# Second expert layer: where expert 1's rows are transposed, and how far the row buffers of the later experts may run ahead

## The chip, the core and the metric

The kernel runs on one core of a Trainium2 chip. The metric is the device time of one execution in microseconds, median of the runs shown. Engines: TensorE (PE), VectorE (DVE), ScalarE (ACT), GpSimd (POOL), SyncE (SP). SP computes nothing here: it issues most of the DMAs, in program order.

## What is computed

The reference is an attention (4 batches, 8 heads, 576 positions, head size 64, with a local window in four heads and a dilated one in the other four), then a first expert layer (8 experts, one expert per token, tokens with a negative skip score are left out), then a second one in which each of the 2304 tokens goes to two of eight experts. The change lies in the second layer:

```python
top2 = np.argpartition(-noisy_logits, 2, axis=1)[:, :2]
...
for e in range(E):                      # E = 8
    for k in range(2):
        mask = top2[:, k] == e
        h = np.maximum(x[mask] @ w1[e], 0.0)          # x: 512 wide, w1[e]: 512 x 1024
        out[mask] += top2_w[mask, k, None] * (h @ w2[e])   # w2[e]: 1024 x 512
```

## The kernel before

**Tiling.** Each expert of the second layer gets 608 slots for its rows, as five tiles: four of 128 rows and one of 96 (`rows2`). fp32 products are made of three passes with operands split into a high and a low part (`mm3`, lines 437 to 441; the split is `split`, lines 431 to 434: ACT writes the high part, DVE or POOL subtracts). For an expert `e` TensorE first makes the hidden values (`hidden2`, line 1437): eight blocks `f`, each in two column ranges `g` (256 and 352 rows), and after each of them ACT and then DVE write the high and low hidden values (lines 1445 and 1446, tiles `hh2`, `hl2`). Then it makes the output of the five row tiles (`product2`, line 1449): 24 matmuls of 512 columns each in one of two `pt` banks, which ACT empties into `y2` (two buffers, line 1460), from where POOL issues a scattered add into the output (line 1216). Expert 0 makes the columns `g` = 1 of its hidden values after the products of its first two row tiles, and expert 7 takes the halves in the other order.

**Rows of an expert.** A tile's rows are gathered by an indirect DMA of POOL (`fetch`, line 1257) into one of four `xg2` buffers. Matmuls need them transposed.
- Expert 0: four TensorE transpositions per tile into a `tp` bank, then a split (`turn`, line 1289).
- Experts 1 to 7: `put` (line 1266) writes the gathered tile to a DRAM tile `xq`, `spread` (line 1273) reads it back with four DMAs of SP into an `xs2` buffer (three of them), 32 partitions each, and `turn_v` (line 1293) transposes blocks of 32 x 32 on DVE into the one `xt2` buffer; the split of that tile follows with the next call. The weights' rows are read in another order for these experts (line 706, `p k` in place of `k p`) so that the permuted rows fit.

**What sets the order.** `P.step` (line 485) cuts the weights into parts between the matmuls; three raw buffers `wraw` are loaded ahead by SP. While expert `e` is worked on, `ready` (line 1505) calls `put`, `fetch` and `spread` for tiles 0 to 2 of expert `e + 1` during its hidden values, and `next_rows` (line 1553) calls `turn_v` and `spread` for the rest during its products, at `f` = 1 and 5. TensorE's order is as written. The order of all other engines is made by a scheduler that takes whatever its model has ready; every engine then works through its own list in order, and an instruction that waits holds up what stands behind it. The `xq` tiles are made anew for each expert, so a `put` waits for no earlier `spread`.

Of the kernel before, what the change touches and what calls it, by code (L numbers as in the profile page):

```python
# [8 lines left out]
F32 = mybir.dt.float32  # L9
# [3 lines left out]
ALU = mybir.AluOpType  # L13
AF = mybir.ActivationFunctionType
# [416 lines left out]
def split(nc, hi, lo, src, eng=None):  # L431

    nc.scalar.activation(hi, src, AF.Copy)  # L433
    (eng or nc.vector).tensor_tensor(out=lo, in0=src, in1=hi.bitcast(F32), op=ALU.subtract)  # L434


def mm3(nc, out, a, b, start, stop):

    nc.tensor.matmul(out, lhsT=a[0], rhs=b[0], start=start, stop=False)  # L439
    nc.tensor.matmul(out, lhsT=a[0], rhs=b[1], start=False, stop=False)  # L440
    nc.tensor.matmul(out, lhsT=a[1], rhs=b[0], start=False, stop=stop)  # L441
# [71 lines left out]
def piece(w1, w2, e, i, dims="o (k p) f -> p (o k) f"):  # L513

    if i < 2:
        src = w1[e:e + 1] if isinstance(e, int) else w1[bass.ds(e, 1)]
        return src.rearrange(dims, p=128)[:, :, 512 * i:512 * i + 512]
    src = w2[e:e + 1] if isinstance(e, int) else w2[bass.ds(e, 1)]
    return src.rearrange("o (f p) d -> p (o f) d", p=128)[:, 4 * (i - 2):4 * (i - 2) + 4, :]
# [3 lines left out]
def tile_attention_moe_moe(ctx, tc, q, k, v, w_skip, w_gate, w1, w2, v_gate, v_noise, noise, u1, u2, out):  # L523
    nc = tc.nc
    B, H, S, D = q.shape
    N, DM = B * S, H * D
    E, F = w_gate.shape[1], w1.shape[2]
# [16 lines left out]
    NS, NA, CAP = 5, 2, 608  # L544
    rows2 = [min(128, CAP - 128 * i) for i in range(NS)]
# [7 lines left out]
    def bank(tag):  # L553
        return ps_pool.tile([128, 512], F32, name=tag, tag=tag, bufs=nbufs[tag])

    cp = ctx.enter_context(tc.tile_pool(name="const", bufs=1))
    dr = ctx.enter_context(tc.tile_pool(name="dr", bufs=1, space=DRAM))
# [141 lines left out]
    every2 = [2, 2, 8, 2, 2, 4, 2, 1]  # L699
    P = Pieces(tc, raw_p)  # L700
    for kk, src in order:
        P.plan(kk, src, every1.get(kk[1]))
    for e in range(E):
        for i in range(4):

            P.plan((2, e, i), lambda e=e, i=i: piece(u1, u2, e, i, f"o ({'p k' if e else 'k p'}) f -> p (o k) f"), every2[e])

    def busy(n):

# [5 lines left out]
    def gather(xg, idx, n):  # L715
        gather.last = nc.gpsimd.indirect_dma_start(out=xg, out_offset=None, in_=xs[:n, :],  # L716
                                                   in_offset=bass.IndirectOffsetOnAxis(ap=idx, axis=0))
        return xg

    def transposed(xg, hi, lo, n=128):  # L720
        ps = bank("tp")
        for c in range(KC):
            nc.tensor.transpose(ps[:, 128 * c:128 * c + n], xg[:n, 128 * c:128 * c + 128], ident[:n, :n])
        split(nc, hi, lo, ps.rearrange("p (c t) -> p c t", c=KC)[:, :, :n])
# [207 lines left out]
    X = {}  # L932
# [30 lines left out]
    for n in range(-LA, NU + LE):  # L963
        a, s, d, e = n + LA, n + LB, n, n - LE
        for op in plan[n].split():
            i = int(op[1]) if len(op) > 1 else 0
# [42 lines left out]
    for f in late(rows_l, 2, KC):  # L1009
# [16 lines left out]
    s_ = slice(LT, NT)  # L1026
# [7 lines left out]
                            in1=rko[:, :, None].to_broadcast([128, T1, E]), op=ALU.is_equal)  # L1034
# [187 lines left out]
    with ExitStack() as lctx:  # L1222
# [34 lines left out]
        def fetch(e, i):  # L1257
            if e < E:
                n = rows2[i]
                j = NS * e + i  # L1260
                xg = xp.tile([128, DM], F32, name="xg2", bufs=4)
                X[e, i] = gather(xg[:n], gidx2[:n, j:j + 1], N if i < NA else SPARE)

        xT2, xq = {}, {}

        def put(e, i):

            if e < E:
                n = rows2[i]
                xq[e, i] = dr.tile([n, DM], F32, name=f"xq{i}")  # L1270
                nc.sync.dma_start(xq[e, i], X.pop((e, i))[:n])

        def spread(e, i):

            if e < E and i < NS:
                g = rows2[i] // 32
                src = xq.pop((e, i)).rearrange("(g r) (q d) -> q r g d", r=32, q=4)
                sh = X[e, i] = ep2[0].tile([128, 4, 128], F32, name="xs2", bufs=3)[:, :g]
                for q_ in range(4):
                    nc.sync.dma_start(sh[32 * q_:32 * q_ + 32], src[q_])  # L1280
# [3 lines left out]
        def place2(e, i):  # L1284
            if i == 0:
                xT2[e] = [xp.tile([128, KC, CAP], F32R, name=n) for n in ("xh2", "xl2")]
            return [x[:, :, 128 * i:128 * i + rows2[i]] for x in xT2[e]]

        def turn(e, i):

            transposed(X.pop((e, i)), *place2(e, i), rows2[i])

        def turn_v(e, i):

            if e < E and i > 0:
                split(nc, *place2(e, i - 1), X.pop((e, i - 1)))
            if e < E and i < NS:
                sh = X.pop((e, i))
                xt = X[e, i] = ep2[0].tile([128, KC, 128], F32, name="xt2", bufs=1)[:, :, :rows2[i]]
                nc.vector.transpose(out=xt.rearrange("p c (g r) -> p g c r", r=32), in_=sh.rearrange("p g (j c) -> p g c j", c=KC))  # L1300

        with ExitStack() as ectx:
# [90 lines left out]
            for op, *t in steps:  # L1393
# [3 lines left out]
                t = int(t[0])  # L1397
# [13 lines left out]
                elif op[0] == "H":  # L1411
                    f = int(op[1])
# [24 lines left out]
        def hidden2(e, hl, f, g):  # L1437
            w = P((2, e, f // 4))
            fs = slice(128 * (f % 4), 128 * (f % 4) + 128)
            s_ = sec[g]  # L1440
            xh, xl = xT2[e]
            ph = bank(("s", "po0", "s", "po1")[2 * (f % 2) + g] if e else ("s", "tp")[f % 2])[:, :s_.stop - s_.start]
            for c in range(KC):
                mm3(nc, ph, (w[0][:, c, fs], w[1][:, c, fs]), (xh[:, c, s_], xl[:, c, s_]), c == 0, c == KC - 1)
            nc.scalar.activation(hl[0][:, f, s_], ph, AF.Relu)  # L1445
            nc.vector.scalar_tensor_tensor(hl[1][:, f, s_], in0=ph, scalar=0.0, in1=hl[0][:, f, s_].bitcast(F32),  # L1446
                                           op0=ALU.max, op1=ALU.subtract)

        def product2(e, hl, i, between=None):
            n = rows2[i]  # L1450
# [50 lines left out]
        def between(i, f):  # L1501
            for g in beside.get((i, f), ()):
                g()

        def ready(e, f):

            for i in {2: (0, 1), 3: (2,), 4: (3,), 7: (4,)}.get(f, ()):
                put(e, i)
            if f == 5:
                fetch(e, NS - 1)  # L1510
            if 4 <= f < 7:
                spread(e, f - 4)

        for e in range(E):
            hl = [ep.tile([128, 8, CAP], F32R, name=nm) for nm in ("hh2", "hl2")] + [[]]
            done = 0
            if e == 0:
                for f in range(8):
                    hidden2(0, hl, f, 0)
                    P.step()  # L1520
                    between(0, f)
                for i in range(NA):
                    product2(0, hl, i, lambda f, i=i: between(1 + i, f))
                    P.step(2)
                for i in range(NS - 1):
                    fetch(1, i)
                for f in range(8):
                    hidden2(0, hl, f, 1)
                    if f >= 6:
                        P.step()  # L1530
                    ready(1, f)
                rest = range(NA, NS)
            elif e + 1 < E:
                for i in range(NS - 1):
                    fetch(e + 1, i)
                for f in range(8):
                    hidden2(e, hl, f, 0)
                    hidden2(e, hl, f, 1)
                    P.step()
                    ready(e + 1, f)  # L1540
                rest = range(NS)
            else:
                for f in range(8):
                    hidden2(e, hl, f, 1)
                for i in range(NA, NS):
                    product2(e, hl, i)
                for f in range(8):
                    hidden2(e, hl, f, 0)
                rest = range(NA)
            xT2.pop(e)  # L1550
            turned = list(range(NS + 1))

            def next_rows(f):
                if f in (1, 5) and turned:
                    t = turned.pop(0)
                    turn_v(e + 1, t)
                    spread(e + 1, t + 3)

            for i in rest:
                product2(e, hl, i, next_rows)  # L1560
                if e == 0 or i + 1 < NS:
                    P.step(2)
# [4 lines left out]
    with tc.If(rest > 0), ExitStack() as ectx:  # L1567
# [36 lines left out]
        with tc.For_i(0, rest1, 1) as i:  # L1604
# [8 lines left out]
            e = nc.sync.value_load(xe1[0:1, bass.ds(i, 1)], min_val=0, max_val=E - 1)  # L1613
# [33 lines left out]
        with tc.For_i(0, rest2, 1) as i:  # L1647
# [14 lines left out]
            e = nc.sync.value_load(xe2[0:1, bass.ds(i, 1)], min_val=0, max_val=E - 1)  # L1662
# [33 lines left out]
```

## Time and profile before

| | us |
|---|---|
| median of 3 runs | 778.08 (777.38 to 780.64) |
| the profiled execution, own time | 777.25 |
| its span, first to last instruction | 775.5 |
| PE busy in the span | 737.2 (95%) |
| DVE, ACT, POOL busy | 390.0, 308.7, 243.4 |

The profile is one execution. "Idle before" names the time in which an engine did nothing ahead of an instruction, and what ended it. A granted clock of 1.00 is TensorE at 2.4 GHz, 0.50 at 1.2 GHz. Expert numbers don't stand in the trace: an expert's stretch is found by the change of TensorE's output from `pt` (products) to `s` and `po` (hidden values).

### The profile page before, as it was taken

What the parts mean: (1) busy time and instruction counts of PE and PEld (TensorE: products, weight loads), DVE (VectorE), ACT (ScalarE), POOL (GpSimd) and SP (SyncE); (2) the same over time, 40 slices, a digit from 0 to 9 for tenths busy, and PEclk for the clock granted to TensorE, in tenths of its full rate; (3) what the DMA queues carried; (4) which work ended last, traced back from release to release, by engine and by line L of the source; (5) the groups of instructions that cost most, each with busy time, mean ns of one, the idle gap of its engine ahead of it and who ended that gap; (6) DMA issues with size and microseconds to landing.
All of it is one profiled execution on the core that took longest, in us unless ns stands there. A gap on an engine that the chain in (4) does not pass through costs nothing.

```text
span 775.5 us, 14491 instructions
## 1 busy us (share of the span) xinstructions
PE 737.2 (95%) x5428; PEld 627.6 (81%) x5428; DVE 390.0 (50%) x1258; ACT 308.7 (40%) x824; POOL 243.4 (31%) x239
## 2 busy tenths in 40 slices
PE   8999989979999999899898999999999999999994
PEld 6876867757977977788796897997997988988883
DVE  7766867827317539837553335553452552250110
ACT  5987753124216153233441442442532443332120
POOL 4322210200032043055525435433322325444011
PEclk9999989998999999999999999999999999999998
DMA  7979565597779996268898788717427445323112
GB/s 189 172 170 255 142 205 190 204 317 259 273 254 327 348 330 221 69 172 237 232 293 241 190 250 246 174 58 156 133 78 150 123 142 96 107 32 44 14 25 30
DMA packets 133420, 138.54 MB, mean 179 GB/s; under 512 B 45184, under 2 KB 85248, under 8 KB 133344
## 3 DMA queue, kind: packets, MB, share of 16 engines
q1 hardware_dynamic: 122224, 113.39, 47.0%
q0 software_dynamic: 9808, 22.86, 15.1%
q10 hardware_dynamic: 1312, 1.31, 0.5%
q8 instruction: 44, 0.72, 0.4%
q14 instruction: 32, 0.26, 0.1%
HBM read 105.22 MB, written 32.31 MB: 177 GB/s over the span
## 4 chain that ended last, share of the span: by engine, by line
PE 66%; DMA 10%; DVE 9%; issue 6%; ACT 6%; SPq 2%; POOL 1%; POOLq 0%; DVEq 0%; ACTq 0%
PE pt L439 8%; PE pt L441 8%; PE pt L440 8%; PE s L746 4%; PE po L439 4%; PE po L441 4%; PE po L440 4%; PE s L439 4%; PE s L440 4%; PE s L441 4%; DMA wraw<-in_moe_w_dram 4%; ACT sm L182 3%; DMA xq<-xg 3%; PE pt L755 3%; PE s L175 2%
## 5 line engine op out<-in xcount | busy, mean ns | idle before, releaser
L439 PE MATMUL pt<-whi,hh 128*128 128x512 f32 (+1 forms) x320 | 127.3, 398 | 3.1 <-ACT y L1460 3.1
L441 PE MATMUL pt<-whi,hl 128*128 128x512 f32 (+1 forms) x320 | 126.7, 396 | 0.0
L440 PE MATMUL pt<-wlo,hh 128*128 128x512 f32 (+1 forms) x320 | 126.6, 396 | 0.0
L434 DVE TENSOR_TENSOR wlo<-wraw,whi 128x512 fp32r<-128x512 f32 x100 | 84.6, 870 | 80.9 <-ACT whi L433 74.5
L434 POOL TENSOR_TENSOR wlo<-wraw,whi 128x512 fp32r<-128x512 f32 x60 | 85.8, 1497 | 120.7 <-ACT whi L433 104.2
L433 ACT ACTIVATE whi<-wraw 128x512 fp32r<-128x512 f32 x160 | 91.2, 622 | 58.5 <-PE po L440 17.1
L716 POOL DMA_INDIRECT xg<-xs,gidx x51 | 51.3, 1006 | 183.7 <-DMA xq<-xg 44.7
L1216 POOL DMA_INDIRECT out_dram<-y,sidx x40 | 62.9, 1573 | 120.7 <-ACT y L1460 117.8
L439 PE MATMUL po<-xh,whi 128*128 128x352 f32 x224 | 73.2, 327 | 2.3 <-DVE hl L1446 2.3
L439 PEld LDWEIGHTS pt<-whi,hh 128*128 128x128 f32 (+1 forms) x320 | 58.8, 184 | 19.0 <-ACT y L1460 4.0
L441 PE MATMUL po<-xh,wlo 128*128 128x352 f32 x224 | 73.0, 326 | 0.0
L440 PE MATMUL po<-xl,whi 128*128 128x352 f32 x224 | 72.9, 325 | 0.0
L439 PE MATMUL s<-xh,whi 128*128 128x256 f32 (+1 forms) x256 | 72.5, 283 | 0.2 <-issue 0.2
L441 PE MATMUL s<-xh,wlo 128*128 128x256 f32 (+1 forms) x256 | 72.5, 283 | 0.0
L440 PE MATMUL s<-xl,whi 128*128 128x256 f32 (+1 forms) x256 | 72.5, 283 | 0.0
L441 PEld LDWEIGHTS pt<-whi,hl 128*128 128x128 f32 (+1 forms) x320 | 58.7, 183 | 15.8
L440 PEld LDWEIGHTS pt<-wlo,hh 128*128 128x128 f32 (+1 forms) x320 | 58.8, 184 | 15.3
L1446 DVE SCALAR_TENSOR_TENSOR hl<-po,hh 128x352 fp32r<-128x352 f32 x56 | 29.3, 522 | 72.9 <-ACT hh L1445 72.8
L1460 ACT ACTIVATE y<-pt,slots 128x512 f32<-128x512 f32 (+1 forms) x40 | 27.3, 682 | 87.0 <-PE pt L441 69.1
L182 ACT ACTIVATE sm<-sm,nmax 128x96 f32<-128x96 f32 x144 | 51.9, 362 | 17.5 <-DVE nmax L178 17.1
L1446 DVE SCALAR_TENSOR_TENSOR hl<-s,hh 128x256 fp32r<-128x256 f32 (+1 forms) x64 | 27.4, 428 | 56.9 <-ACT hh L1445 52.1
L186 POOL TENSOR_TENSOR sm<-sm,rs 128x480 f32<-128x480 f32 (+1 forms) x32 | 29.1, 910 | 76.9 <-DVE nmax L178 52.2
(409 smaller groups left out, 1463.4 us busy)
## 6 DMA issues: line engine op xcount, KB each, us to landing
wraw<-in_moe_w_dram SPq DMA_DIRECT2D x40, 1024.0 KB
whi<-in_moe_w_dram SPq DMA_DIRECT2D x12, 1024.0 KB
wlo<-in_moe_w_dram SPq DMA_DIRECT2D x12, 1024.0 KB
xq<-xg SPq DMA_DIRECT2D x28, 256.0 KB
xs<-xq SPq DMA_DIRECT2D x112, 64.0 KB
out_dram<-zt SPq DMA_DIRECT2D x46, 128.0 KB
xs<-xr SPq DMA_DIRECT2D x13, 256.0 KB
v<-in_v_dram SPq DMA_DIRECT2D x7, 432.0 KB
```

The costliest lines, as they stand in the source:

```text
L182: nc.scalar.activation(sm[:, n, :], sm[:, n, :], AF.Exp, bias=nmax[:, n:n + 1], scale=-1.0, accum_out=ssum[:, n:n + 1])
L186: nc.gpsimd.tensor_tensor(out=sm[:, n0:n1, :], in0=sm[:, n0:n1, :], in1=rs[:, n0:n1, None].to_broadcast([128, n1 - n0, 96]), op=ALU.mult)
L433: nc.scalar.activation(hi, src, AF.Copy)
L434: (eng or nc.vector).tensor_tensor(out=lo, in0=src, in1=hi.bitcast(F32), op=ALU.subtract)
L439: nc.tensor.matmul(out, lhsT=a[0], rhs=b[0], start=start, stop=False)
L440: nc.tensor.matmul(out, lhsT=a[0], rhs=b[1], start=False, stop=False)
L441: nc.tensor.matmul(out, lhsT=a[1], rhs=b[0], start=False, stop=stop)
L716: gather.last = nc.gpsimd.indirect_dma_start(out=xg, out_offset=None, in_=xs[:n, :], in_offset=bass.IndirectOffsetOnAxis(ap=idx, axis=0))
L746: nc.tensor.matmul(ph[:, 128 * f:128 * f + 128], lhsT=w[:, c, 128 * f:128 * f + 128], rhs=self.x[:, c], start=c == 0, stop=c == KC - 1)
L1216: s = nc.gpsimd.indirect_dma_start(out=out, out_offset=bass.IndirectOffsetOnAxis(ap=idx, axis=0), in_=y, in_offset=None, compute_op=ALU.add)
L1446: nc.vector.scalar_tensor_tensor(hl[1][:, f, s_], in0=ph, scalar=0.0, in1=hl[0][:, f, s_].bitcast(F32), op0=ALU.max, op1=ALU.subtract)
L1460: nc.scalar.activation(y[:n], py, AF.Copy, scale=slots2[:n, 2, j:j + 1])
```

## The change

Three things change. The five DRAM tiles `xq` are made once, so that a `put` of one expert must wait until the `spread` of the expert before has read the tile. Expert 1's rows are no longer put, spread and transposed on DVE: `next_rows` of expert 0 calls `turn(1, t)`, four TensorE transpositions per tile between the matmuls of the products, and expert 1's weights are read in the plain order; its last tile is fetched behind the first transposition. For experts 2 to 7, `turn_v` is issued behind the last two hidden-value instructions of the expert at hand, on ACT and on DVE.

```diff
-            P.plan((2, e, i), lambda e=e, i=i: piece(u1, u2, e, i, f"o ({'p k' if e else 'k p'}) f -> p (o k) f"), every2[e])
+            P.plan((2, e, i), lambda e=e, i=i: piece(u1, u2, e, i, f"o ({'p k' if e > 1 else 'k p'}) f -> p (o k) f"), every2[e])
...
-        xT2, xq = {}, {}
+        xT2 = {}
+        xq = [dr.tile([n, DM], F32, name=f"xq{i}") for i, n in enumerate(rows2)]
         def put(e, i):
-            if e < E:
-                n = rows2[i]
-                xq[e, i] = dr.tile([n, DM], F32, name=f"xq{i}")
-                nc.sync.dma_start(xq[e, i], X.pop((e, i))[:n])
+            if 1 < e < E:
+                nc.sync.dma_start(xq[i], X.pop((e, i))[:rows2[i]])
         def spread(e, i):
-            if e < E and i < NS:
+            if 1 < e < E and i < NS:
                 g = rows2[i] // 32
-                src = xq.pop((e, i)).rearrange("(g r) (q d) -> q r g d", r=32, q=4)
+                src = xq[i].rearrange("(g r) (q d) -> q r g d", r=32, q=4)
...
-            nc.scalar.activation(hl[0][:, f, s_], ph, AF.Relu)
-            nc.vector.scalar_tensor_tensor(hl[1][:, f, s_], ...)
+            a = nc.scalar.activation(hl[0][:, f, s_], ph, AF.Relu)
+            d = nc.vector.scalar_tensor_tensor(hl[1][:, f, s_], ...)
+            hidden2.last = a.ins, d.ins
...
-            if f == 5:
+            if f == 5 and e > 1:
                 fetch(e, NS - 1)
...
             def next_rows(f):
                 if f in (1, 5) and turned:
                     t = turned.pop(0)
-                    turn_v(e + 1, t)
+                    if e > 0:
+                        a, d = hidden2.last
+                        with tc.issue_after(a), tc.issue_after(d):
+                            turn_v(e + 1, t)
+                    elif t < NS:
+                        turn(1, t)
+                        if t == 0:
+                            fetch(1, NS - 1)
                     spread(e + 1, t + 3)
```

**DVE at the start of expert 1's hidden values.** `xl2` is the low part of a row tile, `wlo` of weights, `hl2` of hidden values; `xs2_5322` holds tile 0 of expert 2. Before:

```order
L1300 STREAM_TRANSPOSE xt2_5107<-xs2_5036 128x3x4x32
L434 TENSOR_TENSOR xl2_5031<-xt2_5107,xh2_5030 128x4x96
L434 TENSOR_TENSOR wlo_5179<-wraw_4841,whi_5178 128x512 x2
L1300 STREAM_TRANSPOSE xt2_5446<-xs2_5322 128x4x4x32
L434 TENSOR_TENSOR wlo_5317<-wraw_5054,whi_5316 128x512 x2
L1446 SCALAR_TENSOR_TENSOR hl2_5139<-s_5148,hh2_5138 128x256
L434 TENSOR_TENSOR wlo_5317<-wraw_5054,whi_5316 128x512 x2
L1446 SCALAR_TENSOR_TENSOR hl2_5139<-po0_5163,hh2_5138 128x352
```

Now:

```order
L434 TENSOR_TENSOR xl2_4990<-tp_5060,xh2_4989 128x4x128
L434 TENSOR_TENSOR xl2_4990<-tp_5089,xh2_4989 128x4x96
L434 TENSOR_TENSOR wlo_5164<-wraw_4846,whi_5163 128x512 x2
L434 TENSOR_TENSOR wlo_5299<-wraw_5032,whi_5298 128x512 x2
L1445 SCALAR_TENSOR_TENSOR hl2_5124<-s_5133,hh2_5123 128x256
L434 TENSOR_TENSOR wlo_5299<-wraw_5032,whi_5298 128x512 x2
L1445 SCALAR_TENSOR_TENSOR hl2_5124<-po0_5148,hh2_5123 128x352
```

The transposition of expert 2's first tile no longer stands ahead of the first low hidden values; what stands there reads TensorE's banks and weights alone.

**SP around the read-back of expert 2's last two tiles** (`xs2_5448` and `xs2_5471` before, `xs2_5428` and `xs2_5451` now). Before:

```order
L1280 DMA xs2_5448<-xq3_5320 32x4x128 x4
L1271 DMA xq0_5743<-xg2_5637 128x512
L1271 DMA xq1_5745<-xg2_5639 128x512
L1271 DMA xq2_5781<-xg2_5641 128x512
L482 DMA wraw_5531<-in_moe2_w1_dram 128x4x512
L1271 DMA xq3_5817<-xg2_5643 128x512
L1271 DMA xq4_5934<-xg2_5856 96x512
L1271 DMA xq0_6240<-xg2_6134 128x512
L1271 DMA xq1_6242<-xg2_6136 128x512
L1271 DMA xq2_6278<-xg2_6138 128x512
L1271 DMA xq3_6314<-xg2_6140 128x512
L1271 DMA xq4_6431<-xg2_6353 96x512
```

After these twelve rows come one more `put` and then the four DMAs of `xs2_5471`. Now:

```order
L1270 DMA xq0_2761<-xg2_5617 128x512
L1270 DMA xq1_2762<-xg2_5619 128x512
L1270 DMA xq2_2763<-xg2_5621 128x512
L482 DMA wraw_5511<-in_moe2_w1_dram 128x4x512
L1279 DMA xs2_5428<-xq3_2764 32x4x128 x4
L1279 DMA xs2_5451<-xq4_2765 32x3x128 x4
L482 DMA wraw_5585<-in_moe2_w1_dram 128x4x512
L1270 DMA xq3_2764<-xg2_5623 128x512
```

Eleven writes of experts 3, 4 and 5 stood between the two read-backs; now the second follows the first, and both stand behind three writes of expert 3.

**DVE at the start of expert 3's products**, for expert 4's tiles (`xs2_6316` and `xs2_6287` hold its tile 0). Before:

```order
L1446 SCALAR_TENSOR_TENSOR hl2_6133<-po1_6412,hh2_6132 128x352
L434 TENSOR_TENSOR xl2_6460<-xt2_6440,xh2_6459 128x4x128
L1300 STREAM_TRANSPOSE xt2_6463<-xs2_6355 128x4x4x32
L434 TENSOR_TENSOR wlo_6562<-wraw_6276,whi_6561 128x512
L434 TENSOR_TENSOR xl2_6460<-xt2_6463,xh2_6459 128x4x128
```

Now:

```order
L1445 SCALAR_TENSOR_TENSOR hl2_6108<-po1_6383,hh2_6107 128x352
L1299 STREAM_TRANSPOSE xt2_6410<-xs2_6287 128x4x4x32
L434 TENSOR_TENSOR wlo_6532<-wraw_6249,whi_6531 128x512
L434 TENSOR_TENSOR xl2_6430<-xt2_6410,xh2_6429 128x4x128
L1299 STREAM_TRANSPOSE xt2_6433<-xs2_6326 128x4x4x32
L434 TENSOR_TENSOR xl2_6430<-xt2_6433,xh2_6429 128x4x128
```

The transposition of tile 0, which was made a whole expert earlier, now stands behind the last hidden values, ahead of the other four. On TensorE the only difference is five rows of transpositions of expert 1's tiles, between the products of expert 0's last three tiles.

## Rows read from the trace of the kernel before

**Rows 1.** The page: busy time, share and instructions of each engine.
```profile
PE 737.2 (95%) x5428; PEld 627.6 (81%) x5428; DVE 390.0 (50%) x1258; ACT 308.7 (40%) x824; POOL 243.4 (31%) x239
```

**Rows 2.** Busy time by stretch: experts 0 (second half), 1, 2, 3, 6, 7.
```profile
core 0: us, PE busy (x) PEld busy (x) DVE busy (x) ACT busy (x) POOL busy (x), PEclk, DMA share, GB/s
339.43:372.28 32.85, 32.31 (x169) 28.22 (x168) 19.75 (x23) 13.84 (x27) 15.51 (x15) 1.00 0.88 254
372.28:435.87 63.59, 58.40 (x313) 51.21 (x312) 28.54 (x44) 21.83 (x44) 28.21 (x24) 0.95 0.84 234
435.87:491.26 55.39, 54.98 (x314) 48.72 (x313) 25.25 (x36) 21.16 (x42) 26.72 (x23) 1.00 0.85 234
491.26:545.96 54.70, 54.70 (x313) 48.76 (x312) 26.49 (x35) 21.16 (x42) 19.53 (x14) 1.00 0.51 123
...
654.82:709.34 54.52, 54.52 (x314) 48.60 (x312) 16.41 (x26) 21.16 (x42) 27.24 (x21) 1.00 0.30 66
...
709.34:741.69 32.35, 32.35 (x169) 28.56 (x168) 4.20 (x8) 5.78 (x11) 7.81 (x6) 1.00 0.18 23
```

**Rows 3.** Waits by engine, 300 to 500 us: total, times, longest.
```profile
ACT whi L433 <- PE po L440: 5.6, 4, 1.4
...
PE pt L439 <- ACT y L1460: 3.1, 2, 2.7
...
PE po L439 <- DVE hl L1446: 2.3, 1, 2.3
```

**Rows 4.** Timeline of PE: start, us, instruction, idle before it.
```profile
383.35 0.66 PE L439 MATMUL po<-xh,whi 128*128 128x352 f32 x1 [2.34 <-DVE hl L1446]
```

**Rows 5.** Busy time by stretch: transpositions of expert 0; after the two longest waits.
```profile
335.09:338.26 3.17, 3.09 (x21) 2.35 (x20) 1.16 (x2) 1.26 (x3) 2.62 (x2) 1.00 0.65 138
383.34:386.75 3.41, 3.40 (x12) 3.40 (x13) 1.05 (x3) 0.00 (x0) 0.29 (x1) 0.50 0.89 289
424.30:427.71 3.41, 3.41 (x9) 2.64 (x9) 0.00 (x0) 0.00 (x0) 0.59 (x1) 0.50 1.12 250
```

**Rows 6.** Timeline of DVE at the start of expert 1's hidden values.
```profile
376.63 1.12 DVE L1300 STREAM_TRANSPOSE xt<-xs 128x512 f32<-128x512 f32 x1 [3.35 <-DMA xs<-xq]
...
379.18 3.68 DVE L434 TENSOR_TENSOR wlo<-wraw,whi 128x512 fp32r<-128x512 f32 x2
382.78 0.51 DVE L1446 SCALAR_TENSOR_TENSOR hl<-po,hh 128x352 fp32r<-128x352 f32 x1
```

**Rows 7.** Timeline of SP (issues of DMAs) during expert 1.
```profile
401.94 13.41 SPq L1271 DMA_DIRECT2D xq<-xg  x8
415.45 1.84 SPq L1280 DMA_DIRECT2D xs<-xq  x4
```

**Rows 8.** Timelines of DVE and ACT during expert 1's products.
```profile
421.06 0.85 DVE L1300 STREAM_TRANSPOSE xt<-xs 128x384 f32<-128x384 f32 x1 [6.63 <-DMA xs<-xq]
...
422.37 0.67 ACT L1460 ACTIVATE y<-pt,slots 128x512 f32<-128x512 f32 x1
428.94 0.69 ACT L1460 ACTIVATE y<-pt,slots 128x512 f32<-128x512 f32 x1 [5.90 <-DMA out_dram<-y,sidx]
```

**Rows 9.** Timeline of PE: expert 0's transpositions between matmuls.
```profile
335.09 0.60 PE L723 MATMUL tp<-ident,xg 128*128 128x128 f32 x4
...
336.46 0.66 PE L723 MATMUL tp<-ident,xg 128*128 128x128 f32 x4
```

**Rows 10.** Expert 3's products: stretch, then timelines of DVE and ACT.
```profile
518.14:545.96 27.82, 27.82 (x122) 21.88 (x121) 12.60 (x15) 10.21 (x18) 10.60 (x8) 1.00 0.58 121
...
519.50 0.52 DVE L1446 SCALAR_TENSOR_TENSOR hl<-po,hh 128x352 fp32r<-128x352 f32 x1
...
520.65 1.12 DVE L1300 STREAM_TRANSPOSE xt<-xs 128x512 f32<-128x512 f32 x1
...
525.86 0.69 DVE L434 TENSOR_TENSOR xl<-xt,xh 128x512 fp32r<-128x512 f32 x1 [0.70 <-ACT xh L433]
...
529.11 0.86 DVE L1300 STREAM_TRANSPOSE xt<-xs 128x384 f32<-128x384 f32 x1
...
530.43 0.67 ACT L1460 ACTIVATE y<-pt,slots 128x512 f32<-128x512 f32 x1
```

More of the change, by code (lines that the diff above doesn't have):

```diff
@@ L1444, in hidden2 @@
                 mm3(nc, ph, (w[0][:, c, fs], w[1][:, c, fs]), (xh[:, c, s_], xl[:, c, s_]), c == 0, c == KC - 1)
-            nc.scalar.activation(hl[0][:, f, s_], ph, AF.Relu)
-            nc.vector.scalar_tensor_tensor(hl[1][:, f, s_], in0=ph, scalar=0.0, in1=hl[0][:, f, s_].bitcast(F32),
-                                           op0=ALU.max, op1=ALU.subtract)
+            a = nc.scalar.activation(hl[0][:, f, s_], ph, AF.Relu)
+            d = nc.vector.scalar_tensor_tensor(hl[1][:, f, s_], in0=ph, scalar=0.0, in1=hl[0][:, f, s_].bitcast(F32),
+                                               op0=ALU.max, op1=ALU.subtract)
+            hidden2.last = a.ins, d.ins
         def product2(e, hl, i, between=None):
```

## The prediction, made before the changed kernel ran

> **What bounds the kernel now.** I read the page's engine line first: TensorE is busy 737.2 of 775.5 us, 95% [rows 1]. So only two things can change the time: TensorE's idle or slow-clocked stretches, and the work it is given. Next comes the table of stretches, cut where TensorE's output changes from products to hidden values. Experts 3 and 6 take 54.70 and 54.52 us at clock 1.00 [rows 2]; I take 54.6 as the price of an undisturbed expert. Expert 1 takes 63.59 at a mean clock of 0.95, expert 2 takes 55.39, and expert 0's second half 32.85, where the same work of expert 7 (x169 matmuls) takes 32.35 [rows 2]. The loss is therefore in one place: **expert 1**.
>
> The waits name its two causes [rows 3]. TensorE stood 2.3 us for low hidden values of DVE, and 2.7 us for ACT to empty a `pt` bank. After each, TensorE's clock was granted at 0.50 for 3.41 us [rows 5]: the level of 1.2 GHz, at which half of that, 1.7 us, is lost.
>
> - **First stall, 383.35 [rows 4].** DVE's list: it stood 3.35 us, until 376.63, to transpose tile 0 of expert 2, whose read-back hadn't landed; weight parts followed until 382.86 (379.18 plus 3.68), and only then the low hidden values that TensorE wanted [rows 6].
> - **Second stall, ending at 423.09.** ACT's `y` for the bank at 422.37 stood in ACT's list behind the split of expert 2's last tile, which needs DVE's transposition of 421.06, which waited 6.63 us for its read-back [rows 8]. The read-back was late because SP first issued eight `put`s, 13.41 us long, and only then the four reads [rows 7]. They are `put`s of experts far ahead, which fresh `xq` tiles let run.
>
> **The change, part by part.**
>
> *The stalls (gain).* The transposition at 376.63 now stands behind expert 1's last low hidden values, and the early ones of DVE wait for no read-back. The shared `xq` tiles bind a `put` to the read-back of the expert before, so the two late read-backs of expert 2 follow one another on SP, with three writes of expert 3 ahead of them. Three of the eight writes that took 13.41 us are 5.0 us, and they come early. If all disturbed stretches fall to the undisturbed price, expert 1 gives 63.59 - 54.6 = 9.0, expert 2 gives 55.39 - 54.6 = 0.8, expert 0 gives 32.85 - 32.35 = 0.5: together **10.3 us**. The low clock (2 x 1.7) is in it.
>
> *Five transpositions on TensorE (cost).* No row shows one during expert 0's products, but three of the same kind stand between 335.09 and 338.26 [rows 5, 9], 3.17 us from the first group's start. Its 21 instructions are twelve transpositions (three groups of four), seven matmuls of 512 columns, and one matmul that reaches over either edge. A 512-column matmul in a product costs 27.82 / 120 = 0.232 us [rows 10]. So 3.17 - 7 x 0.232 = 1.55 us for three tiles, 0.52 each, **2.6 us** for five. Upper end: the longest group stands at 0.66 [rows 9], 5 x 0.66 = 3.3. Lower end: 0, if they fall into waits that stay. I take 2.6, the nearest row.
>
> *What is removed elsewhere.* Five DVE transpositions (1.12 us each, 0.85 for the last [rows 8, 10]), five writes and twenty reads of SP. DVE, ACT and POOL are busy 50, 40 and 31% [rows 1], and no undisturbed stretch waits for them: **0**. The two splits of each tile stay, now read from a `tp` bank, as expert 0's are.
>
> *New waits of the writes (0).* A `put` on SP now waits for the read-back of the expert before. Its first tiles have about an expert, 54.6 us, of cover. Tile 3 stands close: its read-back goes out two issues ahead. The loaded trip is the one of expert 2's last tile, from the issue's end at 417.29 (415.45 plus 1.84) to DVE's start at 421.06 [rows 7, 8], 3.8 us. So SP may stand 3.8 us, with a load of raw weights queued behind it. These loads are far ahead: what ACT's splits of weights waited for was TensorE giving back old parts, at most 1.4 us at a time [rows 3]. Without that cover it would cost up to 3.8 us once per expert.
>
> *Tile 0's transposition for experts 3 to 7, moved into the products.* It stands ahead of the other four, so that ACT's `y` of row tile 1, which stays behind the split of tile 4, comes later. In expert 3 the last low hidden values end at 520.02 and `y` ends at 531.10 (530.43 plus 0.67) [rows 10]. TensorE needs that bank when row tile 3 starts: 518.14 + 3 x 27.82 / 5 = 534.8 [rows 10]. Slack 3.7 us. The change adds one transposition, 1.12, and the wait for ACT's high part of it, as now at 525.86, 0.70 [rows 10]: 1.8. **1.9 us are left**, so 0.
>
> *Sum.* 10.3 - 2.6 = 7.7 us less. The profiled execution took 777.25, which gives 769.6; the median of the runs shown, 778.08, is 0.83 above it, so **770.4 us**.
>
> **The clock.** Twelve transpositions among seven matmuls ran at a granted clock of 1.00 [rows 5], so the sum has no term for it. The Trainium skill, "TensorE: Matmul & The Clock Gate", section "Part 4: PE-mode transpose", says that a transposition doesn't count as busy for the clock gate as a matmul does. By that rule, the transpositions could pull the clock down, and the time would be that of the third rival below, 778.9; the trace does not agree so far.
>
> **The rivals.**
>
> 1. *A new wait in the products of experts 2 to 6 (slower).* With tile 0 moved, the chain read-back, transposition, split, `y` gets 1.9 us of slack in each. If expert 3's fourth or fifth read-back is later than that, `y` is late and TensorE stands as at 423.09, five times over. The price of that stall was 2.7 idle and 1.7 of low clock, 4.4 us; 5 x 4.4 - 7.7 = 14.3 us slower, **792.4**. It decides the sign from 7.7 / 5 = 1.5 us per expert beyond the slack. For it: the one chain that made the second stall is made longer. Against: what made that late were eight writes, 13.41 us [rows 7], which are gone, and expert 3 ran with all its read-backs in time. Chance 7%.
> 2. *A big stall stays.* The shared tiles move the wait rather than remove it: `put`s that wait, gathers on POOL that wait for their buffers, and scatters behind them, so that ACT's `y` stands for a scatter, as it did for 5.90 us at 428.94 [rows 8]; or DVE's first low hidden values are held up by the weight parts of 3.68 us [rows 6] alone. One stall left costs 4.4: **774.8**, 8%. Both left: 770.4 + 8.8 = **779.2**, and the change then has hardly done what it says, 4%.
> 3. *The clock falls beside the transpositions.* Each fall costs 1.7 us [rows 5]; one after each of the five tiles is 8.5: **778.9**. Against it stands the clock of 1.00 in [rows 5], where the groups came closer together than they will. Chance 4%.
>
> **How the numbers follow.** The forecast has 77%, the rivals 7, 12 and 4. Half a per cent, 3.9 us, is about what a measurement of this kernel can tell from no change: faster is below 774.2, slower above 782.0. The forecast with its bounds lies below 774.2. So does a part of rival 2's first case, which sits on the line at 774.8, and of rival 3, where the clock falls at one or two tiles only (772.1, 773.8): 6% of their 12. The rest of these two and both stalls left are no change, 10%. Rival 1 is slower, 7%. Faster: 77 + 6 = 83%.
>
> The range: the low end is the transpositions hidden in waits, 770.4 - 2.6 = 767.8, less the 0.7 us by which the fastest run shown lies under the median, 767.1. The high end takes in one stall left with the transpositions at 0.66: 774.8 + 0.7 = 775.5. Outside are rival 1, both stalls left, most of rival 3 and some smaller misses of the forecast, about 18%.
>
> **What would show it.** Right: expert 1's stretch near 54.6 us at clock 1.00; the stall at its start and the one in its products gone from the waits; expert 0's products of three row tiles 2.6 us longer than three times 5.56, at clock 1.00; eight writes in a row on SP gone; experts 3 to 6 unchanged at 54.4 to 54.7. The forecast is wrong if TensorE waits for ACT's `y` in the products of experts 2 to 6 (rival 1), if a stretch of clock 0.50 follows a wait in expert 1 (rival 2) or a group of transpositions with no wait before it (rival 3), or if a transposition's group costs far from 0.52 us.

## The result, and the profile after

The changed kernel takes 768.9 us (765.17 to 772.87, 5 runs), the kernel before 779.45 beside it (5 runs): a ratio of 0.9886, interval 0.9852 to 0.9921. Forecast were 770.4 against 778.08, a ratio of 0.990. The profiled execution took 768.6, its span 766.7.

The table of stretches of the changed kernel, cut as in [rows 2]: expert 0's second half, experts 1, 2, 3 and 6, expert 7's half, and at the end expert 0's last three products alone.

```profile
core 0: us, PE busy (x) PEld busy (x) DVE busy (x) ACT busy (x) POOL busy (x), PEclk, DMA share, GB/s
339.11:373.24 34.13, 34.13 (x189) 30.14 (x188) 12.78 (x19) 14.79 (x28) 15.89 (x14) 1.00 0.54 153
373.24:427.76 54.52, 54.52 (x313) 48.60 (x312) 24.78 (x42) 21.27 (x42) 23.05 (x19) 1.00 0.86 239
427.76:482.49 54.73, 54.73 (x313) 48.79 (x312) 23.54 (x36) 21.28 (x42) 21.78 (x17) 1.00 0.62 169
482.49:537.20 54.71, 54.71 (x313) 48.76 (x312) 24.66 (x34) 21.27 (x42) 24.11 (x18) 1.00 0.62 169
646.05:700.58 54.53, 54.53 (x314) 48.60 (x312) 17.82 (x27) 21.27 (x42) 26.92 (x21) 1.00 0.33 71
700.58:732.93 32.35, 32.35 (x169) 28.56 (x168) 4.20 (x8) 5.78 (x11) 7.82 (x6) 1.00 0.18 23
354.47:373.24 18.77, 18.77 (x94) 14.78 (x93) 7.17 (x10) 8.89 (x16) 9.30 (x8) 1.00 0.60 187
```

In every stretch TensorE is busy from end to end at clock 1.00. Expert 1 takes 54.52 where it took 63.59 [rows 2]. Expert 0's half takes 34.13 instead of 32.85: it has 20 more instructions, the transpositions. From expert 0's second half to the end of the span it is 427.6 us (766.7 - 339.11) against 436.1 before (775.5 - 339.43): 8.5 of the span's 8.8 us. I call this **the second layer's time** from here on. It is the better measure: in a second profile of the changed kernel it is 427.6 again, though the layer began 1.8 us earlier. It isn't free of scatter, as one kernel below shows (426.0 and 428.2).

The two stalls are gone. First DVE at the start of expert 1's hidden values, then SP around the read-back of expert 2's last two tiles:

```profile
374.73 1.29 DVE L434 TENSOR_TENSOR wlo<-wraw,whi 128x512 fp32r<-128x512 f32 x2 [1.59 <-issue]
375.94 0.42 DVE L1445 SCALAR_TENSOR_TENSOR hl<-s,hh 128x256 fp32r<-128x256 f32 x1
376.27 1.28 DVE L434 TENSOR_TENSOR wlo<-wraw,whi 128x512 fp32r<-128x512 f32 x2
377.48 0.52 DVE L1445 SCALAR_TENSOR_TENSOR hl<-po,hh 128x352 fp32r<-128x352 f32 x1
```
```profile
387.76 6.20 SPq L1270 DMA_DIRECT2D xq<-xg  x4
394.01 0.55 SPq L482 DMA_DIRECT2D wraw<-in_moe_w_dram  x1
402.89 5.11 SPq L1279 DMA_DIRECT2D xs<-xq  x8
```

The first low hidden values stand behind short weight parts, and no read-back is in DVE's way; compare 376.63 to 382.78 in [rows 6]. Four writes (expert 2's own last tile and three of expert 3, 6.20 us) precede the two read-backs, where eight (13.41 us) preceded the one [rows 7]. The read-backs are now held by something else. In the waits of SP (total, times, longest) they stand 8.3 us for an `xs2` buffer, which comes free when DVE transposes tile 0 of expert 2:

```profile
SPq L1279 <- DVE xt L1299: 9.9, 2, 8.3
```

Nobody waits for them there: DVE transposes these two tiles at 410.21 and 412.72 without a wait.

### The profile page after: what moved, and what is told of

It reads as the page before. It is cut to its first block, busy times and chain, and to the rows that moved or that the text cites. A ratio compares the mean times of both kernels' runs of the same rounds, so it can differ in the third digit from the quotient of the medians.

```text
span 766.7 us, 14489 instructions
## 1 busy us (share of the span) xinstructions
PE 734.3 (96%) x5448; PEld 626.3 (82%) x5448; DVE 379.8 (50%) x1253; ACT 309.2 (40%) x824; POOL 245.9 (32%) x239
## 3 DMA queue, kind: packets, MB, share of 16 engines
q10 hardware_dynamic: 1312, 1.31, 0.5%
## 4 chain that ended last, share of the span: by engine, by line
PE 79%; DVE 7%; DMA 6%; ACT 5%; issue 1%; POOL 1%; SPq 0%; POOLq 0%; DVEq 0%; ACTq 0%
PE pt L439 10%; PE pt L441 10%; PE pt L440 10%; PE po L441 5%; PE po L439 5%; PE po L440 5%; PE s L439 5%; PE s L440 5%; PE s L441 5%; PE s L746 5%; DMA wraw<-in_moe_w_dram 3%; ACT sm L182 3%; PE pt L755 3%; PE s L175 2%; DMA wlo<-in_moe_w_dram 2%; PE tp L146 2%
## 5 line engine op out<-in xcount | busy, mean ns | idle before, releaser
L434 DVE TENSOR_TENSOR wlo<-wraw,whi 128x512 fp32r<-128x512 f32 x100 | 80.8, 833 | 103.5 <-ACT whi L433 95.0
L716 POOL DMA_INDIRECT xg<-xs,gidx x51 | 53.0, 1040 | 157.9 <-PE tp L1192 32.6
```

## The experiments

The change has three parts: **A**, the shared DRAM tiles; **B**, expert 1's rows on TensorE; **C**, the transpositions behind the last low hidden values. I ran the other combinations, then two kernels that separate a cause from its means. The first three columns (us) come from one profile each, the ratio from the runs beside the kernel before on the same chip. Between two profiles of one kernel the second layer's time differs by 0.0, 0.1 and about 2 us (the three kernels profiled twice), so a difference of 2 us between single profiles is weak evidence.

| kernel | expert 0, second half | expert 1 | second layer | ratio, interval |
|---|---|---|---|---|
| before | 32.85 | 63.59 | 436.1 | 1 |
| A | 33.45 | 57.13 | 429.5 | 0.9892 (0.9842 to 0.9942) |
| B | 34.12 | 66.81 | 440.8 | 1.0069 (1.0034 to 1.0104) |
| C | 37.08 | 63.67 | 439.3 | 1.0025 (0.9988 to 1.0062) |
| A, B | 34.13 | 64.36 | 437.3 | 0.9984 (0.9952 to 1.0017) |
| B, C | 34.12 | 72.76 | 445.8 | 1.0138 (1.0092 to 1.0183) |
| A, B, C (the change) | 34.13 | 54.52 | 427.6 | 0.9886 (0.9852 to 0.9921) |
| the same again | 34.12 | 54.52 | 427.6 | 0.9893 (0.9855 to 0.9931) |
| A, C for all tiles | 32.05 | 55.11 | 426.0 | 0.9833 (0.9783 to 0.9882) |
| the same again | 32.05 | 57.34 | 428.2 | 0.9898 (0.9849 to 0.9947) |
| B, C, writes gated | 34.12 | 54.52 | 427.5 | 0.9904 (0.9871 to 0.9937) |
| A, C for all, gathers gated | 32.05 | 54.52 | 425.3 | 0.9865 (0.9818 to 0.9911) |
| the same again | 32.05 | 54.52 | 425.4 | 0.9849 (0.9808 to 0.9891) |

### A alone: the shared tiles

```diff
+        xq = [dr.tile([n, DM], F32, name=f"xq{i}") for i, n in enumerate(rows2)]
...
-                xq[e, i] = dr.tile([n, DM], F32, name=f"xq{i}")
```

> Only the shared DRAM tiles; expert 1 stays on the DVE path and the transpositions are not moved. Theory (the second stall comes from the writes of far experts ahead of the read-back of expert 2's last tile on SP, the first from the early transposition of expert 2's tile 0 on DVE): the second stall goes (2.7 idle and 1.7 at the low clock), the first stays, so expert 1's stretch takes about 59.2 us and the time falls by about 4.8 us from before (with expert 2's 0.4), no cost on TensorE. Rival (what helps is expert 1's rows on TensorE, because that takes traffic away): both stalls stay, time as before. Rival (the moved transpositions do it all): as before.

Measured: second layer 6.6 us less, ratio 0.9892. Expert 1's products take 27.80 us (399.80 to 427.60), so the second stall went with the tiles, as the theory said. The runs can't tell this kernel from the whole change (0.9886). What stays, by the waits of TensorE (total, times, longest) and two stretches at the first stall (the second wait is in expert 0's half):

```profile
PE po L439 <- DVE hl L1445: 2.3, 1, 2.3
PE tp L439 <- DVE hl L1445: 1.1, 1, 1.1
```
```profile
378.79:381.10 2.31, 0.00 (x0) 0.00 (x0) 2.31 (x4) 0.38 (x1) 2.14 (x2) 1.00 0.26 31
381.10:384.50 3.40, 3.39 (x24) 3.39 (x25) 1.58 (x4) 0.47 (x1) 0.30 (x1) 1.00 0.98 309
```

The first stall is as long as before, 2.31 us, but the clock behind it stayed at 1.00: the 3.40 us hold 24 matmuls, where 3.41 us held 12 before [rows 5]. So it costs 2.3 here and cost 4.0 there, and expert 1 took 57.1 instead of the 59.2 that I expected.

### B alone: expert 1's rows on TensorE

```diff
+                    if e > 0:
+                        turn_v(e + 1, t)
+                    elif t < NS:
+                        turn(1, t)
...
```

> Only expert 1's rows on TensorE; DRAM tiles made anew for each expert, transpositions not moved. Theory: eleven writes of far experts still stand ahead of the read-back of expert 2's last tile, so the second stall stays (4.4 us); the first goes, because the read-back of expert 2's tile 0 is issued without expert 1's twenty reads ahead of it; expert 0's products cost 2.1 us more, as in the changed kernel. Expert 1's stretch about 59 us, the time about 2.5 us below before. Rival (the TensorE path alone does it): expert 1's stretch 54.6, time about that of the changed kernel.

Measured: slower by 0.7%, second layer 4.7 us more. Half of the theory fell. The second stall stayed, as expected (expert 1's products 31.30 us, 403.09 to 434.39, with three waits of TensorE for `y`, 3.8 us in all). The first did not go: TensorE stood 7.0 us for low hidden values, three times as long as before. The waits of TensorE and DVE's timeline:

```profile
PE s L439 <- DVE hl L1446: 7.0, 1, 7.0
```
```profile
375.50 1.08 DVE L1300 STREAM_TRANSPOSE xt<-xs 128x512 f32<-128x512 f32 x1 [9.06 <-DMA xs<-xq]
376.50 4.57 DVE L434 TENSOR_TENSOR wlo<-wraw,whi 128x512 fp32r<-128x512 f32 x3
381.00 0.41 DVE L1446 SCALAR_TENSOR_TENSOR hl<-s,hh 128x256 fp32r<-128x256 f32 x1
```

The read-back of expert 2's tile 0 is later, not earlier: DVE gets it 42.0 us after the start of expert 0's second half (375.50, with the stretch beginning at 333.46) where it had it after 37.2 (376.63 [rows 6] and 339.43). And DVE has no transpositions of expert 1 left to do meanwhile, so that 9.06 us of wait stand bare. Why it is later shows on POOL, whose gathers need one of four `xg2` buffers. The gathers of this kernel, and the transpositions on TensorE that give the buffers back (count, shortest, median and longest in ns, first and last start):

```profile
351.98 1.23 POOL L716 DMA_INDIRECT xg<-xs,gidx  x1
...
354.69 0.99 POOL L716 DMA_INDIRECT xg<-xs,gidx  x1 [0.16 <-issue]
...
358.34 0.99 POOL L716 DMA_INDIRECT xg<-xs,gidx  x1 [0.30 <-issue]
```
```profile
L723 PE MATMUL tp<-ident,xg x20: 243/271/273, 350.2 to 363.3; 128*128 128x128 f32 x16, 96*128 96x96 f32 x4
```

The first of these three fetches expert 1's last tile, the next two expert 2's first. So expert 2's rows are asked for 21.2 us after the start of the stretch (354.69 - 333.46). In the kernel before, `put` empties the same buffers early, and the gather went out at 349.78, 10.4 us after the start:

```profile
349.78 1.00 POOL L716 DMA_INDIRECT xg<-xs,gidx  x1 [0.31 <-ACT whi L433]
```

B holds expert 1's gathered rows until TensorE comes to them, and with them the buffers that expert 2 needs. (The times fit this; POOL's own list, with splits of weights between the gathers, may have a part in it.)

### C alone: the transpositions moved

```diff
-                    turn_v(e + 1, t)
+                    if e > 0:
...
+                        a, d = hidden2.last
+                        with tc.issue_after(a), tc.issue_after(d):
+                            turn_v(e + 1, t)
...
```

(For the tiles of expert 2 and later, as in the change; expert 1's stay where they were.)

> Only the transpositions of experts 2 to 7 moved behind the last low hidden values. Theory: the first stall goes (2.3 idle, 1.7 at the low clock); the second stays or grows, since ten writes now stand ahead of the read-backs of both of expert 2's last tiles. Expert 1's stretch about 59 us, the time about 4 us below before, no cost on TensorE. Rival (the order alone does it, because the y of row tile 1 now stands ahead of the split of expert 2's last tile on ACT): expert 1's stretch 54.6, time about 9 us below before.

Measured: ratio 1.0025, no difference that the runs can tell; second layer 3.2 us more. The waits:

```profile
PE pt L439 <- ACT y L1461: 6.5, 1, 6.5
PE tp L439 <- DVE hl L1446: 3.2, 1, 3.2
```

The first stall went, as the theory said (hidden values 26.72 us, 375.99 to 402.71), but the time did not fall by 4 us. The second stall grew from 2.7 to 6.5, with twelve writes of later experts ahead of the two read-backs (I had counted ten). I had not expected the third: the transposition of expert 1's own tile 0 stood before expert 0's low hidden values, and TensorE stood 3.2 us where it had stood 0.54 before. Behind these 3.2 us the mean granted clock was 0.58 for 3.4 us, so expert 0's half took 37.08; behind the 6.5 it was 0.50 for as long.

### A and C for all tiles: no transposition on TensorE

```diff
-                    if e > 0:
+                    if True:
...
-                    elif t < NS:
-                        turn(1, t)
-                        if t == 0:
-                            fetch(1, NS - 1)
...
```

(The edit is against the changed kernel and lets `turn_v` with its `issue_after` serve expert 1 too; the conditions `1 < e` and the order of expert 1's weights go back too.)

> Shared DRAM tiles and moved transpositions, for expert 1's tiles too, which stay on the DVE path: no transposition is added on TensorE. Theory (tiles and order remove the stalls, TensorE's transpositions are only a cost): expert 1's stretch 54.6, expert 0's second half near 32.3, and the time about 2 us below the changed kernel, some 10.5 us below before. Rival (expert 1's rows had to leave the DVE path, because its tiles are late themselves): TensorE waits in expert 0's products or at the start of expert 1, 2 to 5 us, and the time is that of the changed kernel or 3 us above.

> Shared tiles and moved transpositions, no transposition of expert 1's rows on TensorE, once more, beside the changed kernel on the same chip. Theory: 1.6 us less than the changed kernel in the second layer (2.1 less in expert 0's products, 0.6 more in expert 1's hidden values). Rival (the first reading was the chip's scatter): no difference between the two.

Measured: 426.0 us in one profile, 428.2 in the other, against 427.6 of the changed kernel. The first fits the theory; the forecast made from it, 1.6 less once more, failed. Expert 0's half is 32.05 in both, 2.08 below the changed kernel, so **the price of the five tiles on TensorE is 2.08 us**. Expert 1 took 55.11 and 57.34, though: TensorE stands at its start, 0.1 us in the first profile and 2.3 in the second, as the first rival had it. The second profile, first ACT, then DVE, then POOL:

```profile
372.66 0.69 ACT L1460 ACTIVATE y<-pt,slots 96x512 f32<-96x512 f32 x1 [2.65 <-DMA out_dram<-y,sidx]
373.24 1.14 ACT L433 ACTIVATE whi<-wraw 128x512 fp32r<-128x512 f32 x2
```
```profile
373.89 2.71 DVE L434 TENSOR_TENSOR wlo<-wraw,whi 128x512 fp32r<-128x512 f32 x2 [3.68 <-ACT whi L433]
376.53 0.41 DVE L1445 SCALAR_TENSOR_TENSOR hl<-s,hh 128x256 fp32r<-128x256 f32 x1
```
```profile
360.85 0.92 POOL L716 DMA_INDIRECT xg<-xs,gidx  x1 [1.80 <-DMA xq<-xg]
...
364.59 1.62 POOL L1216 DMA_INDIRECT out_dram<-y,sidx  x1 [0.30 <-issue]
```

ACT's `y` of the last row tile waits for a `y2` buffer, that is, for the scatter of row tile 2. That scatter stands on POOL behind gathers of expert 2 that wait for their buffers. Behind `y` on ACT stand expert 1's weights, behind those DVE's low parts and hidden values: this is the prediction's second rival, as a small case. In the first profile `y` stood too, for 1.99 us.

### A and B without C, B and C without A

The first leaves out C of the changed kernel (`turn_v` without `issue_after`), the second A (a new `xq` tile for each expert and row tile).

> The change without its third part: shared DRAM tiles and expert 1's rows on TensorE, the transpositions of experts 2 to 7 not moved. Theory (each stall has its own cause: the tiles cure the one in expert 1's products, the moved transpositions the one at the start of its hidden values): the products of expert 1 take 27.8, and TensorE waits some 7 us at the start of expert 1, as with expert 1's rows on TensorE alone, plus 1.7 at the low clock; the time is about 8.7 us above the changed kernel, near 777.5. Rival (with shared tiles the read-back of expert 2's tile 0 comes early enough): no wait, the time of the changed kernel.

> The change without its first part: DRAM tiles made anew for each expert, expert 1's rows on TensorE, transpositions moved. Theory: no wait at the start of expert 1; the read-backs of expert 2's last two tiles stand behind twelve writes of far experts, so TensorE waits 6 to 7 us in expert 1's products and then loses 2 to 4 us at the low clock; the time is about 9 us above the changed kernel, near 778. Rival (expert 1 off the DVE path leaves the queue enough room): products of expert 1 take 27.8, the time of the changed kernel.

Measured: 437.3 and 445.8 us, ratios 0.9984 and 1.0138. Both stalls sit where the theory puts them. Without C, TensorE waits once, 7.1 us, for DVE's low hidden values, and the products of expert 1 take 27.80 (408.40 to 436.20). Without A, it waits once too, but 16.0 us instead of 6 to 7; fourteen writes of later experts, not twelve, stand ahead of the read-backs. SP, DVE and ACT of that kernel (B, C):

```profile
387.42 16.20 SPq L1271 DMA_DIRECT2D xq<-xg  x7
405.09 18.81 SPq L1271 DMA_DIRECT2D xq<-xg  x8
424.00 3.94 SPq L1280 DMA_DIRECT2D xs<-xq  x8
```
```profile
430.01 1.08 DVE L1300 STREAM_TRANSPOSE xt<-xs 128x512 f32<-128x512 f32 x1 [20.31 <-DMA xs<-xq]
```
```profile
431.12 0.63 ACT L433 ACTIVATE xh<-xt 128x512 fp32r<-128x512 f32 x1 [22.14 <-DVE xt L1300]
431.65 0.67 ACT L1461 ACTIVATE y<-pt,slots 128x512 f32<-128x512 f32 x1
```
```profile
432.38:436.00 3.62, 3.62 (x9) 2.85 (x10) 1.53 (x3) 0.52 (x1) 1.58 (x1) 0.50 1.02 276
```

The chain reads from the top: seven writes in 16.20 us (one of them expert 2's own last tile) and eight in 18.81, then the read-backs, then DVE, which stood 20.31 us for them, then ACT's split, and only behind that the `y` for which TensorE waits. The clock was then 0.50 for 3.62 us. The waits of SP and POOL from 385 to 430 us (total, times, longest) show why writes are slow:

```profile
SPq L1271 <- DMA xg<-xs,gidx: 26.5, 9, 7.8
POOL xg L716 <- DMA xq<-xg: 25.1, 8, 10.9
```

A write waits for its gather, and a gather for a buffer that an earlier write empties.

### The changed kernel again

> The changed kernel once more, beside the next one on the same chip. Theory: as its first profile, second layer from expert 0's second half to the end 427.6 us with no wait of TensorE; what differs from run to run lies ahead of it, at TensorE's wait near 168 us, which took 2.4 to 4.9 us in the profiles so far.

Measured: ratio 0.9893, second layer 427.6, no wait of TensorE in it. The second layer began at 337.30 us instead of 339.11, and TensorE's wait near 168 us took 3.5 us instead of 4.9. Over all the profiles of this study that wait was 1.4 to 4.9 us long (1.4 with B alone, which the expectation left out). It doesn't explain all of the scatter, and I have not followed the rest, which lies ahead of the change.

### The order without the wait

B and C with a new tile for each expert, but each write issued behind the read-back of the same tile of the expert before:

```diff
+                with ExitStack() as gate:
+                    if (e - 1, i) in read:
+                        gate.enter_context(tc.issue_after(read[e - 1, i].ins))
                     nc.sync.dma_start(xq[e, i], X.pop((e, i))[:n])
...
-                    nc.sync.dma_start(sh[32 * q_:32 * q_ + 32], src[q_])
+                    read[e, i] = nc.sync.dma_start(sh[32 * q_:32 * q_ + 32], src[q_])
```

> The change with DRAM tiles made anew for each expert, but each write issued behind the read-back of the same tile of the expert before: SP's order of writes and read-backs is then that of the changed kernel, and no write waits for a read-back. Theory (what the shared tiles do is to hold SP's order, not the wait itself): no wait of TensorE in expert 1, second layer 427.6 us, the time of the changed kernel, some 18 us below the same kernel without the gate. Rival (the writes' waits on shared tiles matter, or the memory they use): a wait in expert 1's products stays, several us.

Measured: second layer 427.5 us, expert 1 54.52, ratio 0.9904. SP of this kernel:

```profile
384.87 3.49 SPq L1274 DMA_DIRECT2D xq<-xg  x4
388.45 1.18 SPq L482 DMA_DIRECT2D wraw<-in_moe_w_dram  x1
399.91 5.10 SPq L1283 DMA_DIRECT2D xs<-xq  x8
```

The same four writes, load and eight reads as in the changed kernel, and 18.3 us less than the kernel without the gate. What the shared tiles do is hold SP's order; that a write waits for a read (11.4 us of SP's time in the changed kernel from 335 to 740 us, 2.7 at most at once) costs and gives nothing.

### A better version

A and C for all tiles, and the gathers of expert 2 behind the scatter of expert 0's row tile 2:

```diff
+                with ExitStack() as gate:
+                    if e == 1:
+                        gate.enter_context(tc.issue_after(hl0[2][NA].ins))
+                    for i in range(NS - 1):
+                        fetch(e + 1, i)
```

> No transposition added on TensorE, shared tiles, all transpositions moved, and the gathers of expert 2 issued behind the scatter of expert 0's row tile 2. Theory (the 2.3 us wait that the kernel without this gate showed at the start of expert 1 in one of two profiles comes from y of row tile 4 on ACT, which stood for that scatter and held expert 1's weights up): expert 0's second half 32.05, expert 1 54.5, second layer 425.4 us in every profile, 2.2 below the changed kernel. Rival (the wait is chance in the transfers): a wait of some 2 us again.

> The same kernel once more, for its profile: second layer 425.4 us again, if the gate removes the cause.

Measured: 425.3 and 425.4 us, expert 1 at 54.52 in both, no wait of TensorE in the second layer. ACT at the same place as above now:

```profile
367.71 2.18 ACT L433 ACTIVATE whi<-wraw 128x512 fp32r<-128x512 f32 x4
369.87 0.68 ACT L1460 ACTIVATE y<-pt,slots 96x512 f32<-96x512 f32 x1
```

`y` follows the weights without a wait. The wait of `y` that the theory names is gone, and TensorE's with it; two profiles are few to exclude chance. By the profiles this kernel beats the changed one by 2.2 us, 0.3%. Its ratios, 0.9865 and 0.9849, lie below the changed kernel's 0.9886 and 0.9893, but the intervals overlap, so the runs' times alone don't show it; the kernel without the gate has 0.9833 and 0.9898.

## Why the prediction was right

- **What bounds the kernel, and the undisturbed price.** Right. Expert 1 takes 54.52, forecast 54.6; experts 3 and 6 are unchanged within 0.01.
- **The gain, 10.3 us.** Right, 10.5: expert 1 gave 9.07, expert 2 0.66, expert 0 0.80 (32.85 to 32.05, read from the kernels without B). My yardstick for expert 0 was expert 7's half, 32.35; the true floor was 0.3 lower.
- **First stall: ended by C; second stall: ended by A.** Both right: C alone ends the first and A alone the second, and the change without C has a wait of 7.1 us at the first place, without A one of 16.0 at the second. The forecast took the sum of the two as if they were free to add. They are not: by one profile each, A alone gives 6.6, B alone and C alone lose 4.7 and 3.2, and all three together give 8.5.
- **What made the first stall.** Half seen. The two weight parts that DVE worked on until 382.86 [rows 6] ran while POOL split weights:

```profile
379.17 2.53 POOL L434 TENSOR_TENSOR wlo<-wraw,whi 128x512 fp32r<-128x512 f32 x2
```

They took 3.68 us there and take 1.28 now, when POOL's split comes later, at 382.02. Without these 2.40 us the low hidden values would, as an estimate, have ended at 380.9 (382.78 + 0.51 - 2.40 [rows 6]), before TensorE ran out of work at 381.01 (383.35 - 2.34 [rows 4]). By this estimate the stall needed both the late transposition and the meeting with POOL; C brings DVE's parts forward and so ends both. The second rival has the 3.68 us, but not where they come from.
- **Five transpositions, 2.6 us.** Oversized: 2.08, or 0.42 a tile. The price per tile, 0.52, came from a stretch [rows 5] with a wait in it: the weight load of the second group stood for its gathered rows. The matmul ahead of that group, then the load:

```profile
335.99 0.40 PE L441 MATMUL pt<-whi,hl 128*128 128x512 f32 x1
```
```profile
336.46 0.42 PEld L723 LDWEIGHTS tp<-ident,xg 128*128 128x128 f32 x4 [0.52 <-DMA xg<-xs,gidx]
```

The group began 0.47 us after that matmul [rows 9], where 0.23 is usual. Without these 0.24 us the same sum gives 1.31 for three tiles, 0.44 each, 2.2 for five. B is not what ends a stall: the runs of the kernel without it (0.9833 and 0.9898) are no slower, and by itself it makes expert 2's rows late. Without B, though, TensorE waited up to 2.3 us until the gathers were gated.
- **What is removed elsewhere, and new waits of the writes, 0.** Right. No wait of TensorE in the second layer. A write waited 2.7 us at most for a read-back; up to 3.8 was allowed for. That read-backs would stand 8.3 us for an `xs2` buffer was not foreseen, and cost nothing.
- **Tile 0 moved, 1.9 us of slack left in experts 3 to 7.** Right; I looked at expert 3 alone, and TensorE waits in no other. There, ACT's `y` of row tile 1 and TensorE's first matmul in the bank that it frees:

```profile
523.56 0.67 ACT L1460 ACTIVATE y<-pt,slots 128x512 f32<-128x512 f32 x1
```
```profile
526.06 0.39 PE L439 MATMUL pt<-whi,hh 128*128 128x512 f32 x1
```

`y` ends at 524.23, and the bank is taken at 526.06: **1.8 us**. The first rival's mechanism is real, as the kernel with B and C shows with 16.0 us in expert 1; in the changed kernel the read-backs are in time.
- **The second rival** did not come in the changed kernel. It came, as 2.3 us, in the kernel without B.
- **The clock.** 1.00 in the stretch that holds the five tiles' transpositions (354.47 to 373.24). The Trainium skill, "TensorE: Matmul & The Clock Gate", section "Part 4: PE-mode transpose", says that a transposition doesn't count as busy as a matmul does. With four of them to twelve matmuls, no run here shows a fall by that rule.
- **The sum.** 10.5 - 2.1 = 8.4 by these sizes, 8.5 measured in the second layer, 7.7 forecast. The measured median, 768.9, lies inside the forecast range, 767.1 to 775.5. It is 10.55 us below the median beside it; the change explains 8.5 of these, and the other 2 are scatter that I haven't followed.

## What to carry to other kernels

A queue in program order pays for buffers that let one producer run far ahead: fewer buffers, or one line that orders the write behind the read, gave 18 us here beside B and C, without any engine doing less; fewer buffers alone gave 6.6. Work that is moved to another engine keeps its input buffers until that engine comes to it: ask who waits for them. Parts of a change should be tried alone and left out one by one: here B loses on its own, C gains nothing that the runs can tell, and B was only a cost once the gathers were gated.

## What was not expected of the hardware

**The clock after a wait.** A wait of the same length had two prices. After TensorE had stood 2.33 us in the kernel before, its clock was granted at 0.50 for 3.41 us [rows 4, 5]. After 2.31 us in the kernel with A alone, and after 2.33 us in one profile of A and C for all tiles, it stayed at 1.00. What TensorE had done ahead of each wait looks alike by its busy time (4.35 of 4.51 us before, 4.49 of 4.49 with A alone). Nor does the fall always come at the wait's end: the low clock began with the first matmul behind the first stall, but 1.2 us behind the end of the second (424.30 [rows 5] against 423.09). So 1.7 us of such a stall's 4.0 can come and go, and I don't know what decides it.

**Two engines that split weights at once.** A weight part of DVE that met a split on POOL took 2.95 us in place of 0.65, and ended only after POOL's. In the kernel before, DVE and POOL:

```profile
352.43 0.65 DVE L434 TENSOR_TENSOR wlo<-wraw,whi 128x512 fp32r<-128x512 f32 x1
...
353.43 2.95 DVE L434 TENSOR_TENSOR wlo<-wraw,whi 128x512 fp32r<-128x512 f32 x1
```
```profile
353.29 2.53 POOL L434 TENSOR_TENSOR wlo<-wraw,whi 128x512 fp32r<-128x512 f32 x2
```

From 300 us on, in all thirteen profiles, no DVE part without such company took more than 0.71 us; beside POOL's split some took 0.65 and the longest 5.60. The first stalls of the kernels with A, with B and with both have it too: 3.68 us for two parts, 4.57 and 4.64 for three. So it matters here when DVE gets to its weights, and not only how many it has.
